# Fused soft-capped attention and maxout layer on one core: row-wise loads of v, a fourth U buffer, the weight product earlier, and the last sums of exp on VectorE

## The chip, the core and the metric

The kernel runs on one core of a Trainium2 chip. The time of a run is the device time of that core, in microseconds (us). A run more than 1.5% above the fastest of the same kernel counts as slow and is left out of ratios. Small differences are read from ratios of many runs; profiles, of which there is one for each kernel, show where time goes. TensorE multiplies matrices, ScalarE does tanh and exp, VectorE and GpSimd add, copy, convert and scale, and SP issues DMAs. The span is the time from the first to the last instruction of a profile, and the granted clock is the share of TensorE's full clock that the profile records.

## The reference, cut to what matters

```python
# q, k, v: (8 batches, 12 heads, 448 tokens, 64), float32
scores = 30 * tanh((q @ k.T) / 8 / 30)
attn = exp(scores) / sum(exp(scores))      # max subtraction cancels; |scores| <= 30
x = (attn @ v)                             # heads side by side: (3584, 768)
out = maximum(x @ w1, x @ w2) @ w_out      # d_ff = 1024, out (3584, 768)
```

The kernel uses max(h1, h2) = h2 + relu(h1 - h2). With wd = w1 - w2 and M = w2 @ w_out, out = x @ M + relu(x @ wd) @ w_out. It computes wd and M itself, in its first third.

## The kernel before

Two heads are one pair (48 pairs), two pairs are one **quad** (24, the loop's `t`), three pairs are one group, for which q, k and v are loaded together. A batch needs three quads. While quad `t` is in its attention part, TensorE also works off **fillers**: single matmuls of the second stage, taken from a queue with `F(n)`. A batch of 132 or 160 such matmuls (`moe(b)`) enters the queue when the rows of that batch are normalized. Line numbers in profiles are those of the kernel that ran; after the change most are 5 higher (`L396` becomes `L401`).

```python
def F(n):                        # let up to n fillers out
    while n > 0 and fill_q: ...  # an empty queue loses the quota

def pv(t, ab):                   # attn @ v of one pair, and the sums of exp
    ...
    if ab:
        ss = pv_psum.tile([P, 512], f32, name="ss")
        for m in range(2):
            nc.tensor.matmul(ss[64 * m : 64 * m + 64, :S], ones2, expo[t, 2][:, m, :],
                             start=True, stop=False)                       # L340
        nj = NJ if t < NS else 1
        for j in range(nj):
            for m in range(4):   # 12 matmuls before quad NS; 4 on VectorE's sums (esum) from NS on
                x = e_of(t, m // 2, j)[:, m % 2, :] if t < NS else esum[t][:, m, :]
                nc.tensor.matmul(ss[32 * m : 32 * m + 32, :S], ones, x,
                                 start=False, stop=(j == nj - 1))          # L347
    ...
    if ab == 0:
        U[t] = upool.tile([P, 2, S], f32, name="u", bufs=3)
    nc.vector.tensor_copy(U[t][:, ab, :], ps[:, :S])                       # L351

def normalize(t, ab, eng=nc.gpsimd):     # xT = U * 1/sum, on GpSimd       # L383
    ...

for t in range(NQ):
    i = 2 * t
    weights(i)                           # M: turn_w2 and premultiply enter the queue, from MS on
    if t % 3 == 2 and t > 2:
        fill_q.append(moe(t // 3 - 1))   # its first matmuls, L396, read xT of quads up to t - 3
    scores(t + 1, 0); ex(t, 3)
    F(2); add(t, 0, 1); F(2)             # add: sums of exp on VectorE
    ...
    F(5 + more8 if more else 0)
    if t > 4: spread(t - 2)              # 1/sum back from memory (rec_b), on the SP queue
    extra(i)                             # loads (SP), casts (GpSimd), DMA transposes (SP) of later groups
    F(6 if more else 3)
    scores(t + 1, 1); ex(t + 1, 0)
    pv(t, 0)
    F(8 + more8); F(3 if more else 0)
    if MS < i <= MS + KC: subtract(i - MS - 1)    # wd
    if t > 4: normalize(t - 2, 0); normalize(t - 2, 1)
    ...
```

A denominator goes a long way: sums on TensorE, copy (VectorE), DMA, reciprocal (VectorE), DMA to memory (`rec_d`), DMA back to all rows (`rec_b`), multiplication on GpSimd (`xT`). All these DMAs are issued by SP, in order, among the loads of q, k, v and the transposes. A batch has six chunks `c`, one for each pair; its first matmuls read chunks 0 to 3, so only four of them can run if the last quad of the batch isn't normalized.

## Time and profile before

| | before |
|---|---|
| median of the runs at hand before the prediction | 376.99 us (376.53 to 381.85, 3 runs) |
| profiled run | 380.94 us, span 379.2 us, granted clock 0.98 |
| TensorE / ScalarE / VectorE / GpSimd busy | 92% / 74% / 53% / 40% |
| ScalarE waits for scores (tanh, L296) | 31.1 us |
| attention part ends (last exp) | about 319 us; then TensorE alone |

A quad needs 11.8 us of ScalarE. What exceeds this in a quad is a wait somewhere. I therefore time quads: from the first matmul of the first `pv` of one quad to that of the next.

Three waits of the kernel before (the view of waits: engine, line, what it waited for; us in total, times, longest):

```profile
POOL kqf L178 <- DMA qr<-in_q_dram: 9.4, 9, 2.2
...
PE s L295 <- DMA qkT<-kqf: 2.3, 2, 1.9
PE mm L396 <- POOL xT L383: 1.3, 1, 1.3
```

GpSimd's cast of q (`kqf`) waits 9.4 us in all for its loads and never over 2.2, TensorE's scores wait twice for a DMA transpose (`qkT`), and the first matmuls of a batch wait once for the normalized rows (`xT`).

### The profile page before, as it was taken

To read this page: it belongs to the slowest core of one execution; us is meant where nothing else is said; L and a number is where in the kernel's file an instruction comes from. 1 tells how busy PE (TensorE), PEld (TensorE's weight loads), DVE (VectorE), ACT (ScalarE), POOL (GpSimd) and SP (SyncE) were. 2 spreads that over 40 slices of the span, in tenths; PEclk is the share of its full clock that TensorE was granted. 3 is DMA by queue.
4 is the path that set the end of the run, shared out by engine and by line. 5 is a ranking of instruction groups with operands and counts; after the bars stand their busy time and mean duration, and the time that the engine had idled before them with its cause. 6 is when DMAs were issued, how large, how long until landed. Compare 5 with 4: busy or idle time off the path is not lost.

```text
span 379.2 us, 6549 instructions
## 1 busy us (share of the span) xinstructions
PE 349.0 (92%) x2492; PEld 168.2 (44%) x2492; DVE 200.6 (53%) x348; ACT 281.8 (74%) x265; POOL 150.1 (40%) x188
## 2 busy tenths in 40 slices
PE   3677986898999999999999999999989999999996
PEld 2223443443444444444444454434434444555563
DVE  4223473567665676455745654557448556633421
ACT  4999986697999989998898899889958897000000
POOL 3734135637554445444562456243644302420000
PEclk9997898999999999999999999999989999999999
DMA  7999999996788987999698959896988132422022
GB/s 251 263 209 220 274 284 223 227 193 139 215 212 221 213 232 203 223 234 255 177 213 208 251 163 250 232 242 165 216 217 213 51 91 105 122 80 95 2 83 84
DMA packets 104464, 71.56 MB, mean 189 GB/s; under 512 B 58224, under 2 KB 99440, under 8 KB 104432
## 3 DMA queue, kind: packets, MB, share of 16 engines
q1 hardware_dynamic: 102480, 67.99, 71.1%
q0 software_dynamic: 1952, 3.15, 4.5%
q8 instruction: 19, 0.31, 0.4%
q14 instruction: 13, 0.11, 0.1%
HBM read 53.48 MB, written 11.18 MB: 171 GB/s over the span
## 4 chain that ended last, share of the span: by engine, by line
PE 65%; DMA 19%; DVE 5%; SPq 4%; ACT 3%; issue 2%; POOL 1%; POOLq 0%; DVEq 0%; ACTq 0%
PE mm L396 17%; PE mm L411 16%; PE mm L408 12%; PE pv L334 6%; DMA qkT<-kqf 6%; PE s L295 6%; DMA qr<-in_q_dram 6%; DMA vr<-in_v_dram 4%; DMA rec_b<-rec_d 3%; PE pv L348 3%; PE ss L347 2%; PE s L290 1%; DVE u L351 1%; ACT expo L303 1%; ACT tanh L296 1%
## 5 line engine op out<-in xcount | busy, mean ns | idle before, releaser
L296 ACT ACTIVATE tanh<-s 128x896 bf16<-128x896 f32 x144 | 124.3, 915 | 32.5 <-PE s L295 31.1
L303 ACT ACTIVATE expo<-tanh 128x1792 bf16<-128x1792 bf16 (+1 forms) x96 | 144.9, 1510 | 0.1
L383 POOL TENSOR_TENSOR xT<-u,rec_b 128x448 bf16<-128x448 f32 x48 | 58.4, 1238 | 101.1 <-DMA rec_b<-rec_d 81.2
L411 PE MATMUL mm<-wo_sb,gT 128*128 128x384 bf16 x448 | 86.8, 330 | 0.0
L396 PE MATMUL mm<-xT,wd_sb 128*128 128x448 bf16 x384 | 79.1, 354 | 2.7 <-POOL xT L383 1.3
L351 DVE COPY u<-pv 128x448 f32<-128x448 f32 x48 | 29.9, 624 | 91.0 <-PE pv L348 78.3
L408 PE MATMUL mm<-wm_sb,xT 128*128 128x384 bf16 x336 | 66.6, 326 | 0.2 <-DVE gT L400 0.2
L411 PEld LDWEIGHTS <-gT 128*128 128x128 bf16 x448 | 43.6, 99 | 31.1 <-issue 3.6
L415 DVE COPY osb<-mm 128x384 f32<-128x384 f32 x56 | 31.1, 555 | 46.3 <-PE mm L411 46.0
L396 PEld LDWEIGHTS <-wd_sb 128*128 128x128 bf16 x384 | 37.2, 98 | 38.4 <-issue 5.9
L295 PE MATMUL s<-qkT 64*128 64x448 bf16 x288 | 43.2, 371 | 11.1 <-ACT tanh L298 3.4
L400 DVE TENSOR_SCALAR gT<-mm 128x448 bf16<-128x448 f32 x64 | 39.1, 616 | 16.8 <-PE mm L396 16.6
L408 PEld LDWEIGHTS <-xT 128*128 128x128 bf16 x336 | 32.5, 98 | 23.3 <-issue 1.9
L334 PE MATMUL pv<-expo,vp 128*64 128x448 bf16 x288 | 37.5, 370 | 0.0
L158 POOL CAST vp<-vr 128x1152 bf16<-128x1152 f32 x15 | 18.0, 1201 | 46.8 <-DMA vr<-in_v_dram 43.5
L321 DVE TENSOR_TENSOR esum<-esum,expo 128x896 bf16<-128x896 bf16 x38 | 29.9, 787 | 1.5
L319 DVE TENSOR_TENSOR esum<-expo 128x896 bf16<-128x896 bf16 x38 | 26.6, 699 | 0.0
L295 PEld LDWEIGHTS <-qkT 64*128 64x128 bf16 x288 | 9.4, 95 | 36.8 <-issue 28.7
L298 ACT ACTIVATE tanh<-s 128x896 bf16<-128x896 f32 x24 | 22.0, 917 | 4.4 <-PE s L290 3.9
L334 PEld LDWEIGHTS <-vp 128*64 128x64 bf16 x288 | 12.4, 110 | 21.3 <-issue 15.2
L232 PE MATMUL mm<-wo_sb,w2T 128*128 128x384 bf16 x96 | 19.1, 334 | 1.4 <-DVE qkT L264 1.4
L178 POOL CAST kqf<-qr 128x1152 bf16<-128x1152 f32 x12 | 14.5, 1207 | 9.6 <-DMA qr<-in_q_dram 9.4
(56 smaller groups left out, 227.7 us busy)
## 6 DMA issues: line engine op xcount, KB each, us to landing
rec_b<-rec_d SPq DMA_DIRECT2D x48, 224.0 KB
kr<-in_k_dram SPq DMA_DIRECT2D x12, 576.0 KB
qr<-in_q_dram SPq DMA_DIRECT2D x12, 576.0 KB
vr<-in_v_dram SPq DMA_DIRECT2D x12, 576.0 KB
out_dram<-osb SPq DMA_DIRECT2D x17, 384.0 KB
out_dram<-osb SPq DMA_DIRECT2D x22, 192.0 KB
osb<-in_moe_w_dram SPq DMA_DIRECT2D x6, 512.0 KB
vr<-in_v_dram SPq DMA_DIRECT2D x8, 288.0 KB
```

Source lines behind the costliest of these rows:

```text
L295: nc.tensor.matmul(s[:, h, :S], k0[r, j * P : (j + 1) * P], qTn[r, :])
L296: nc.scalar.activation(tanh[t, p][:, 2 * m : 2 * m + 2, :], s[:, :, :S], AF.Tanh, scale=scale / cap)
L303: nc.scalar.activation(expo[t, p], tanh[t, p][:, 0:n, :], AF.Exp, scale=float(cap))
L321: nc.vector.tensor_add(d, d, e_of(t, ab, 0 if ab else 2))
L334: nc.tensor.matmul(ps[r, :S], vp[g % 2][:, 2 * n + h, j, :], e_of(t, ab, j)[:, h, :], start=(j == 0), stop=False)
L351: nc.vector.tensor_copy(U[t][:, ab, :], ps[:, :S])
L383: eng.tensor_mul(xT[b // 2][:, hp, cs], U[t][:, ab, :], rec[t][:, ab, :])
L396: nc.tensor.matmul(ps[:, :S], wd_sb[:, c, f * P : (f + 1) * P], x[:, c, cs], start=(c == 0), stop=(c == KC - 1))
L400: nc.vector.tensor_relu(g[:, f, cs], ps[:, :S])
L408: nc.tensor.matmul(ps[:, : DM // 2], x[:, c, ts], wm_sb[:, c, hs], start=(c == 0), stop=False)
L411: nc.tensor.matmul(ps[:, : DM // 2], g[:, f, ts], wo_sb[:, f, hs], start=False, stop=(f == FC - 1))
L415: nc.vector.tensor_copy(osb[:, hs], ps[:, : DM // 2])
```

## The change

Its intent: take matmuls from TensorE (the sums of the tokens left over, 64 of 448, of both pairs), take away the stall of VectorE at the third U tile, finish M and the first batch sooner, have the transposes of even groups half a quad earlier, and load v of the first groups in longer rows. The diff, cut to its core:

```diff
-        if g < NT and what == "v":          # 4 DMAs per group: gone; the cast sorts the rows
[...]
-        if step == 0:
+        if step == 2:                        # left tokens of a pair: 64 partitions
+            r = slice(64 * ab, 64 * ab + 64)
+            d = esum[t][r, ab::2, :]
+            nc.vector.tensor_add(d, d, expo[t, 2][r, :, :])
+        elif step == 0:
[...]
-            for m in range(2):
+            for m in range(2 if t < NS else 0):
[...]
-            U[t] = upool.tile([P, 2, S], f32, name="u", bufs=3)
+            U[t] = upool.tile([P, 2, S], f32, name="u", bufs=4)
[...]
-    NS = 5
+    NS = 2
[...]
-            at(e - 4, cross, g)              # DMA transpose of group g
+            at(e - 4 if g % 2 or first else e - 5, cross, g)
[...]
-    MS = 3
+    MS = 2                                   # and the loads of w1, w2 sooner
[...]
-        if t % 3 == 2 and t > 2:
+        if t % 3 == 2 and t > 5:
             fill_q.append(moe(t // 3 - 1))
[...]
-        if t > 4:
+        if t > 3:
             spread(t - 2)                    # likewise normalize, half a quad sooner for quad 2
[...]
+        if t == 4:                           # in the middle of quad 4
+            fill_q.append(moe(0))
[...]
+        add(t, 0, 2)
         F(2 + more8 if more else 0)
-        add(t, 1, 0)
+        add(t, 1, 2)
```

## The prediction

> **What bounds the kernel now.** I read the page first, then the chain of waits, then the idle times of ScalarE and VectorE in order of time, then the PE timeline of the end.
>
> The page and the groups of instructions:
>
> ```profile
> PE 349.0 (92%) x2492; PEld 168.2 (44%) x2492; DVE 200.6 (53%) x348; ACT 281.8 (74%) x265; POOL 150.1 (40%) x188
> PE   3677986898999999999999999999989999999996
> ACT  4999986697999989998898899889958897000000
> L296 ACT ACTIVATE tanh<-s 128x896 bf16<-128x896 f32 x144 | 124.3, 915 | 32.5 <-PE s L295 31.1
> L321 DVE TENSOR_TENSOR esum<-esum,expo 128x896 bf16<-128x896 bf16 x38 | 29.9, 787 | 1.5
> L340 PE MATMUL ss<-expo,ones 128*64 128x448 bf16 x48 | 8.8, 362 | 0.0
> ```
>
> There are two stages. Until the last exp (319 us) ScalarE is almost full; then TensorE alone works off what is left of the second product (319 to 376 us). ScalarE's own pace in a stretch without gaps (148.63 to 160.42 us in the timeline) is 11.8 us for a quad (two head pairs). From the first pv matmul of quad 5 (90.30 us) to that of quad 22 (309.32 us) a quad takes 219.0/17 = 12.9 us, so about 1.05 us per quad, 18 us in all, is ScalarE waiting for scores because TensorE has not come to them. Before that the largest gaps are in quads 3 to 5. ScalarE's timeline, and VectorE's and TensorE's at the same places (the bracket is the idle time before and what ended it):
>
> ```profile
> 63.33 0.62 DVE L351 COPY u<-pv 128x448 f32<-128x448 f32 x1 [5.60 <-POOL xT L383]
> 67.98 1.73 ACT L296 ACTIVATE tanh<-s 128x896 bf16<-128x896 f32 x2 [4.26 <-PE s L295]
> ...
> 76.11 1.73 ACT L296 ACTIVATE tanh<-s 128x896 bf16<-128x896 f32 x2 [1.45 <-PE s L295]
> ...
> 90.28 1.73 ACT L296 ACTIVATE tanh<-s 128x896 bf16<-128x896 f32 x2 [2.14 <-PE s L295]
> ```
>
> ```profile
> 277.61 0.55 PE L295 MATMUL s<-qkT 64*128 64x448 bf16 x4 [1.85 <-DMA qkT<-kqf]
> 278.08 1.73 ACT L296 ACTIVATE tanh<-s 128x896 bf16<-128x896 f32 x2 [2.33 <-PE s L295]
> ...
> 283.00 1.73 ACT L296 ACTIVATE tanh<-s 128x896 bf16<-128x896 f32 x2 [1.62 <-PE s L295]
> ```
>
> The first says: the copy of quad 3's product into its U tile stood 5.6 us until GpSimd had normalized quad 0, because there are three U tiles; VectorE is in order, so TensorE's evacuations stood behind it, then the scores, then ScalarE. The second: the DMA transpose of an even group came late, TensorE stood 1.85 us, and ScalarE lost 2.33 and then 1.62 us. Smaller gaps behind transposes of even groups are 0.62 us (161.04) and 0.93 us (237.98).
>
> **What the Trainium skill says.** "VectorE: DVE Perf Modes", The perf-mode tier table: a two-input bf16 op in SBUF runs at two elements per cycle, and the page measured some 150 cycles fixed cost; for 896 elements (150 + 448)/0.96 GHz = 0.62 us, an estimate. The trace agrees: undisturbed adds take 0.61 to 0.62 us; the means of 699 and 787 ns hold adds of up to 1.55 us, in stretches where GpSimd was at work. It also says that lanes run in parallel along the free dimension, so an add on 64 partitions should cost the same as one on 128; no view of this kernel has one. "TensorEngine Tiling (Array Packing)", Key Properties: changing the tiling mode drains TensorE. The trace agrees in this: a pair of 64-column sum matmuls ought to stream 448 columns at 2.4 GHz, 0.19 us, but takes 0.29 us from start to start of the next group. "TensorE: Matmul & The Clock Gate", Part 1: an idle TensorE falls to half clock. After the 1.85 us stall, 8 matmuls of L411 take 2.56 us in the chain, against 1.30 us elsewhere; this is why one late transpose cost ScalarE twice. "DMA: Bandwidth & Descriptors", Specifications: under 512 bytes a transfer is below line rate. The page shows 58224 of 104464 packets under 512 bytes, with the DMA share at 0.94 to 1.14 in the first 60 us; the trace doesn't show how much of that the size of the packets costs.
>
> **The change part by part.** The end of the attention stage:
>
> ```profile
> 315.23 0.76 PE L334 MATMUL pv<-expo,vp 128*64 128x448 bf16 x6
> 315.82 0.36 PE L340 MATMUL ss<-expo,ones 128*64 128x448 bf16 x2
> 316.11 0.37 PE L347 MATMUL ss<-esum,ones 128*32 128x448 bf16 x4
> 316.42 0.36 PE L348 MATMUL pv<-expo,vl 128*128 128x448 bf16 x1
> ```
>
> *Sums on VectorE.* L340 is gone for quads 2 to 23: 316.11 - 315.82 = 0.29 us of TensorE each. In quads 2, 3, 4 the twelve L347 matmuls (82.25 to 82.94 us, 0.69 us) become four (0.31 us), 0.38 us more each. Together 22 x 0.29 + 3 x 0.38 = 7.5 us of TensorE. VectorE gets 2 adds of 0.62 to 0.79 us in 22 quads, and 4 more in quads 2 to 4: 56 adds, 35 to 44 us; it goes from 201 to about 240 us, 65% of the span. Where does this lie? In quads 5 to 22 TensorE is the later one, by about 0.4 us in a quad of L408 and L411 matmuls (12.2 us against 11.8) and 1.3 to 1.8 us in one of L396 (13.2 to 13.6 us; each of the 48 fillers takes 0.189 instead of 0.163 us). So 0.29 us per quad counts in full in some 14 quads (those from 8 on): 4 us. VectorE has the room: in the densest stretch (168 to 171 us, an L396 quad) one extra add falls between the evacuations and the sum matmul; the last add ended at 170.12 us and would end about 170.8 us, the sum matmul stands at 171.25 us. If GpSimd stretches adds to 1.1 us, half a microsecond is lost; I take off 1 us over all these quads. In quads 2 and 3 it is tighter: per quad 2 subtractions (2.5 us), 2 w2T and 4 wm copies (3.6), 2 qkT copies (1.3), U, sums and reciprocal (2.3) make 9.7 us, and six adds of 0.75 us make 14.2 us against 11.8 us of ScalarE. I expect 1 to 2 us lost in each.
>
> *Four U tiles.* Takes away the 5.6 us stall of VectorE, so ScalarE's 4.26 us and the cold clock's 0.81 us behind it. With a fourth tile the copy of quad 4 (at 77.29 us) meets a normalization finished at 63.3 us: hidden.
>
> *M sooner.* I counted fillers from the loop: TensorE's quotas that find an empty queue are 82 before (44 in quad 0, 36 in 1, 2 in 2) and 76 after (44, 18, and 14 in quad 7, where the second batch can't begin before quad 8). So the tail has 295 matmuls in place of 301: 6 x 0.163 = 1.0 us. The first L396 matmul moves from quad 5 to the second half of quad 4, and so does its wait for the normalization of quad 2. Before, this and the last wd_sb, wm_sb waits cost 2.14 us in quad 5 and 1.45 us at 76 us; since the spread of the sums also moves half a quad ahead, I expect about 1.5 us to remain of these 3.6.
>
> *Transposes of even groups half a quad ahead.* Removes 2.33 + 1.62 + 0.62 + 0.93 = 5.5 us at best; the SP queue is in order and stands behind sums and casts, so I count 4.
>
> *v in 1792-byte rows.* For four groups 4 DMAs become 1, and 1152 packets (768 of 768 bytes, 384 of 256) become 384. At the mean 42 ns per packet (71.1% of 16 x 379 us over 102480 packets) the old way is an estimated 3.0 us of all engines per group; the new packets are longer, so perhaps 0.5 us is saved per group. ScalarE waits for no v load from 11 to 54 us, so little reaches the end. The casts get dearer: GpSimd 4 x about 0.66 (from 64x192 in 0.35 us and 64x384 in 0.50 us) + 2 x 0.35 = 3.3 us instead of 1.8, three times, in a stage where it works some 6 of 20 us; on VectorE about 1 us more at 17 us. I count this part as 0, within 0.5 us.
>
> Sum: 5 (U) + 2 (first L396) + 4 (transposes) + 4 - 1 (sums in steady state) + 1 (tail) + about 0.5 (last quad) - 3 (VectorE in quads 2, 3) = 12.5 us. Not all such gaps add up, since removing one lets the next wait come forward; I keep 11: 377 - 11 = 366 us.
>
> **Rivals.** (1) VectorE becomes what TensorE waits for, through the two mm banks and the sum matmul that now waits for six adds. For it: the adds stretched to 1.55 us, and the 14.2 us in quads 2 and 3; against it: 53% busy, and gaps of 0.4 to 1.3 us in each quad of the timeline. It would give back 5 to 8 us: about 372. (2) ScalarE's pace takes it all: whatever TensorE saves is hidden behind tanh and exp. For it: at 100 to 130 us ScalarE has no gap. Against it: 18 us of gaps after quad 5. If only the U stall and the transposes were won: about 368. (3) The SP queue and the DMAs: the earlier transpose blocks the loads and sums behind it, and a stall only moves. For it: SP waits of 31 us for rec_d and 12 us for casts of q, and DMA at 0.8 to 1.0. It would leave about 371. (4) Everything works, and the wait for the first L396 vanishes: about 361.
>
> **Range and chances.** 80%: 360 to 373. The threshold for faster is 377 x 0.98 = 369.4; rivals 1 and 3 land above it, the sum itself well below. Faster 0.72, within 2% 0.25, slower 0.03 (it would need VectorE to lose more than all gaps hold).
>
> **What would show it.** L340 with only 4 matmuls, and sums in quads 2 to 4 shorter; adds on VectorE near 132 with a mean of 0.7 to 0.8 us; no U copy waiting for xT near 63 us; ScalarE's waits for scores down from 31 to 17 to 20 us; the last exp at about 308 instead of 319 us; the tail 1 us shorter; no wait for qkT at quad 20. Wrong, if VectorE's waiting shows as new idle time of TensorE ("DVE esum", "DVE gT") of over 3 us, or if ScalarE's gaps stay near 30 us.

## More of the kernel before

Runs of one kernel differ by a few microseconds: the kernel before took between 375.5 and 384.7 us in all its runs, on several chips.

Since the loop puts scores and fillers of quad t before `pv(t, 0)`, a batch that enters at the top of quad 8 begins in what is timed as quad 7.

## The result, and the profile after

| | before | after |
|---|---|---|
| median | 377.60 us (376.53 to 381.85, 4 runs) | 390.81 us (389.89 to 395.53, 4 runs) |
| ratio of fast runs, 95% interval | | 1.0353 (1.0238 to 1.0469): slower |
| profiled run | 380.94 us, span 379.2 | 389.89 us, span 388.1 |

A ratio is the mean time of one kernel's fast runs over that of the other's of the same rounds, so it is not quite the ratio of the medians that stand beside it.

The page of the kernel after: busy times, TensorE and ScalarE in 40 slices of the span, and the groups that answer to those of before:

```profile
PE 348.1 (90%) x2424; PEld 165.7 (43%) x2424; DVE 249.8 (64%) x407; ACT 281.7 (73%) x265; POOL 162.9 (42%) x197
...
PE   4677877688999499999999999999999999899996
...
ACT  4999985837899859998899899998997897000000
...
L296 ACT ACTIVATE tanh<-s 128x896 bf16<-128x896 f32 x144 | 124.3, 914 | 40.2 <-PE s L295 39.1
...
L326 DVE TENSOR_TENSOR esum<-esum,expo 128x896 bf16<-128x896 bf16 x44 | 37.0, 842 | 2.1
...
L322 DVE TENSOR_TENSOR esum<-esum,expo 64x896 bf16<-64x896 bf16 x44 | 34.9, 793 | 0.9
L324 DVE TENSOR_TENSOR esum<-expo 128x896 bf16<-128x896 bf16 x44 | 33.1, 752 | 0.0
```

TensorE is busy for about as long as before and stands longer. VectorE has 49 us more. ScalarE waits 39.1 us for scores in place of 31.1. The slices, 9.7 us each, show where: a trough in slices 6 to 10 (49 to 97 us), where ScalarE has 8, 5, 8, 3 and 7 tenths and TensorE 7, 7, 6, 8 and 8; a single 4 of TensorE in slice 14 (126 to 136 us) with ScalarE's 5 behind it; then 9s of TensorE almost throughout.

The share of each engine in the chain that ended last, of the kernel before:

```profile
PE 65%; DMA 19%; DVE 5%; SPq 4%; ACT 3%; issue 2%; POOL 1%; POOLq 0%; DVEq 0%; ACTq 0%
```

And of the kernel after:

```profile
PE 69%; DVE 19%; ACT 5%; DMA 3%; issue 2%; POOL 1%; SPq 0%; DVEq 0%; POOLq 0%
```

VectorE, which was 5% of the chain, is 19% of it. DMA, which was 19%, is 3%: the chain runs no longer through loads, but through adds and copies. The quads, in us, from the starts of the pv matmuls:

| quad | 2 | 3 | 4 | 5 | 7 | 13 | 14 | 19 | 20 | last pv at |
|---|---|---|---|---|---|---|---|---|---|---|
| before | 12.87 | 18.53 | 14.17 | 12.59 | 11.98 | 12.36 | 13.65 | 15.85 | 14.11 | 319.0 |
| after | 17.70 | 19.51 | 14.48 | 13.10 | 17.46 | 12.74 | 13.31 | 13.46 | 13.43 | 327.7 |

The spans differ by 388.1 - 379.2 = 8.9 us: +1.5 up to the start of quad 2, +5.8 in quads 2 and 3, +0.6 in quads 4 to 6, +5.5 in quad 7, -4.7 in quads 8 to 22, +0.2 after that. So there are two holes and a gain behind them.

**The first hole, quads 2 and 3.** One stretch of each kernel, two quads long (columns: stretch; length; busy us and number of instructions of TensorE, its weight loads, VectorE, ScalarE, GpSimd; granted clock; DMA share; GB/s). Beside after I set the experiment e3 below, which has the four U tiles but no adds in these quads, since the kernel before has its U stall here. Of after:

```profile
46.19:83.40 37.21, 27.81 (x263) 13.27 (x261) 28.23 (x40) 23.55 (x23) 22.66 (x24) 0.88 0.69 200
```

And of e3:

```profile
44.27:70.89 26.62, 23.81 (x280) 12.05 (x278) 17.25 (x27) 23.67 (x24) 14.33 (x16) 1.00 1.04 276
```

VectorE's 28.2 us are just the 2 x 14.2 us that the prediction had counted. But the two quads took 37.2 us and not 28.2. Compare e2 below, which differs from e3 in the adds alone (VectorE 29.95 us in 36.15 us): of 12.7 us more work on VectorE 9.5 us came through as length, although e3's VectorE had 9.4 us idle. TensorE's timeline of after says why (each line: start, length, engine, line, operation, and in the bracket the idle time before it and what ended it):

```profile
54.38 0.37 PE L352 MATMUL ss<-esum,ones 128*32 128x448 bf16 x2 [1.51 <-DVE esum L326]
...
59.89 0.60 PE L262 MATMUL mm<-ident,kqf 64*64 64x64 bf16 x26 [2.52 <-DVE wm_sb L237]
...
68.97 1.46 PE L232 MATMUL mm<-wo_sb,w2T 128*128 128x384 bf16 x8 [1.48 <-DVE qkT L264]
...
76.99 0.60 PE L262 MATMUL mm<-ident,kqf 64*64 64x64 bf16 x26 [2.62 <-DVE w2T L224]
```

TensorE stands for a sum, and for copies (`wm_sb`, `qkT`, `w2T`) that stand in VectorE's order behind adds and subtractions; then it is VectorE that waits for TensorE's next product (in the same stretch 3.6 us for L232, 3.8 us for pv), and the idle times of the two add up. The granted clock falls too: it is 0.50 from 60.53 to 63.94 us and from 77.60 us to the end of the stretch, 0.88 on average, where e3 has 1.00; in the first of these, 6 matmuls of L232 take 2.08 us in place of 1.14. One add shows how long such a stand can be; VectorE and GpSimd in the timeline, and then ScalarE's gap:

```profile
73.63 2.70 DVE L324 TENSOR_TENSOR esum<-expo 128x896 bf16<-128x896 bf16 x1
73.64 2.21 POOL L388 TENSOR_TENSOR xT<-u,rec_b 128x448 bf16<-128x448 f32 x2
...
83.19 1.73 ACT L296 ACTIVATE tanh<-s 128x896 bf16<-128x896 f32 x2 [6.30 <-PE s L295]
```

The add took 2.70 us where one alone takes 0.61. It began within 0.01 us of GpSimd's two normalizations and ended, at 76.33 us, 0.48 us after the second of them (73.64 + 2.21 = 75.85 us). It is the longest add of the profile; what all such blocking costs was not measured.

**The second hole, quad 7.** SP, GpSimd, TensorE and ScalarE in order of time:

```profile
119.39 4.51 SPq L268 DMA_TRANSPOSE qkT<-kqf  x1
123.96 0.57 SPq L125 DMA_DIRECT2D qr<-in_q_dram  x1
...
129.39 1.15 POOL L178 CAST kqf<-qr 128x1152 bf16<-128x1152 f32 x1 [5.66 <-DMA qr<-in_q_dram]
...
133.04 2.22 POOL L388 TENSOR_TENSOR xT<-u,rec_b 128x448 bf16<-128x448 f32 x2 [1.58 <-DMA rec_b<-rec_d]
...
134.22 0.53 PE L401 MATMUL mm<-xT,wd_sb 128*128 128x448 bf16 x1 [2.26 <-POOL xT L388]
135.31 4.07 PE L401 MATMUL mm<-xT,wd_sb 128*128 128x448 bf16 x11 [0.56 <-POOL xT L388]
...
139.77 1.73 ACT L296 ACTIVATE tanh<-s 128x896 bf16<-128x896 f32 x2 [4.92 <-PE s L295]
```

A transpose holds SP for 4.51 us; the load of q comes behind it, and so do the sums and rec_b; GpSimd stands 5.66 us for q, then for rec_b; and TensorE, which has just begun the second batch, has nothing else to do and stands 2.26 and 0.56 us. Its clock is low as well: the granted clock is 0.50 from 132.21 to 139.04 us, and 11 matmuls take 4.07 us (11 of the 13 in a row take 2.24 us in e18 below). It fell 0.25 us into the first of these waits, after 3.41 us in which TensorE had been busy for 1.83. ScalarE loses 4.92 us. The waits of after, in the same form as those of before:

```profile
POOL kqf L178 <- DMA qr<-in_q_dram: 26.7, 9, 5.7
...
PE mm L401 <- POOL xT L388: 3.7, 4, 2.3
```

No wait for `qkT <- kqf` by DMA is left on TensorE. In its place GpSimd waits 26.7 us for q and TensorE 3.7 us for xT.

### The profile page after: what moved, and what is told of

Same layout as the page of the kernel before. It is cut to its first block, busy times and chain, and to the rows that moved or that the text cites.

```text
span 388.1 us, 6456 instructions
## 1 busy us (share of the span) xinstructions
PE 348.1 (90%) x2424; PEld 165.7 (43%) x2424; DVE 249.8 (64%) x407; ACT 281.7 (73%) x265; POOL 162.9 (42%) x197
## 4 chain that ended last, share of the span: by engine, by line
PE 69%; DVE 19%; ACT 5%; DMA 3%; issue 2%; POOL 1%; SPq 0%; DVEq 0%; POOLq 0%
PE mm L416 17%; PE mm L401 14%; PE mm L413 13%; PE s L295 7%; PE pv L339 7%; PE pv L353 3%; DVE esum L322 3%; DVE esum L324 3%; DVE esum L326 2%; ACT expo L303 2%; PE mm L232 2%; PE ss L352 2%; ACT tanh L296 2%; DVE u L356 2%; DVE gT L405 2%
## 5 line engine op out<-in xcount | busy, mean ns | idle before, releaser
L296 ACT ACTIVATE tanh<-s 128x896 bf16<-128x896 f32 x144 | 124.3, 914 | 40.2 <-PE s L295 39.1
L388 POOL TENSOR_TENSOR xT<-u,rec_b 128x448 bf16<-128x448 f32 x48 | 60.5, 1280 | 91.2 <-DMA rec_b<-rec_d 80.8
L401 PE MATMUL mm<-xT,wd_sb 128*128 128x448 bf16 x384 | 81.8, 359 | 6.5 <-POOL xT L388 3.7
L295 PE MATMUL s<-qkT 64*128 64x448 bf16 x288 | 44.0, 376 | 11.3 <-DVE qkT L264 4.8
L405 DVE TENSOR_SCALAR gT<-mm 128x448 bf16<-128x448 f32 x64 | 39.1, 614 | 16.6 <-PE mm L401 16.2
L326 DVE TENSOR_TENSOR esum<-esum,expo 128x896 bf16<-128x896 bf16 x44 | 37.0, 842 | 2.1
L339 PE MATMUL pv<-expo,vp 128*64 128x448 bf16 x288 | 37.5, 369 | 0.0
L322 DVE TENSOR_TENSOR esum<-esum,expo 64x896 bf16<-64x896 bf16 x44 | 34.9, 793 | 0.9
L324 DVE TENSOR_TENSOR esum<-expo 128x896 bf16<-128x896 bf16 x44 | 33.1, 752 | 0.0
L178 POOL CAST kqf<-qr 128x1152 bf16<-128x1152 f32 x12 | 14.5, 1208 | 27.0 <-DMA qr<-in_q_dram 26.7
L158 POOL CAST vp<-vr 128x1152 bf16<-128x1152 f32 x12 | 14.9, 1246 | 23.9 <-DMA vr<-in_v_dram 20.4
L232 PE MATMUL mm<-wo_sb,w2T 128*128 128x384 bf16 x96 | 21.3, 360 | 2.9 <-DVE qkT L264 2.9
```

The costliest lines, as they stand in the source:

```text
L295: nc.tensor.matmul(s[:, h, :S], k0[r, j * P : (j + 1) * P], qTn[r, :])
L296: nc.scalar.activation(tanh[t, p][:, 2 * m : 2 * m + 2, :], s[:, :, :S], AF.Tanh, scale=scale / cap)
L322: nc.vector.tensor_add(d, d, expo[t, 2][r, :, :])
L324: nc.vector.tensor_add(d, e_of(t, ab, 1 if ab else 0), e_of(t, ab, 2 if ab else 1))
L326: nc.vector.tensor_add(d, d, e_of(t, ab, 0 if ab else 2))
L339: nc.tensor.matmul(ps[r, :S], vp[g % 2][:, 2 * n + h, j, :], e_of(t, ab, j)[:, h, :], start=(j == 0), stop=False)
```

## The experiments

Three first suspicions, lettered in the expectations where letters are used: **A**, the adds from quad 2 on take too much of VectorE while M is prepared; **B**, M and the first batch come before their inputs; **C**, the earlier transposes hold up the SP queue. Two more came up on the way: **E**, the order of SP's issues is what makes xT late; **F**, what decides is how many fillers of the previous batch are left when a batch begins. The median before in each row is over all runs of the kernel before in the same batch of runs on that chip; the ratio uses those of the same rounds. Each edit is given against the kernel named.

| run | median us (range, runs) | before us | ratio (95%) |
|---|---|---|---|
| e1 | 390.32 (387.68 to 393.63, 4) | 379.79 | 1.0219 (1.0141 to 1.0297) |
| e2 | 387.05 (386.72 to 387.56, 4) | 379.79 | 1.0157 (1.0087 to 1.0226) |
| e3 | 378.76 (376.81 to 384.15, 20) | 379.79 | 1.0010 (0.9979 to 1.0040) |
| e4 | 388.96 (387.57 to 395.24, 4) | 379.79 | 1.0194 (1.0122 to 1.0267) |
| e5 | 379.22 (375.43 to 383.29, 20) | 379.29 | 0.9965 (0.9935 to 0.9996) |
| e6 | 381.60 (377.90 to 385.56, 20) | 379.29 | 1.0056 (1.0028 to 1.0084) |
| e7 | 379.49 (376.12 to 383.79, 12) | 379.29 | 1.0010 (0.9971 to 1.0050) |
| e8 | 380.39 (378.09 to 383.95, 20) | 379.29 | 1.0032 (1.0004 to 1.0059) |
| e9 | 396.88 (393.90 to 573.32, 4) | 379.28 | 1.0456 (1.0368 to 1.0545) |
| e10 | 381.64 (379.86 to 387.15, 8) | 379.28 | 1.0072 (1.0030 to 1.0114) |
| e11 | 385.55 (383.93 to 390.14, 4) | 379.28 | 1.0169 (1.0117 to 1.0221) |
| e12 | 386.07 (381.32 to 386.95, 4) | 379.28 | 1.0172 (1.0098 to 1.0245) |
| e13 | 397.33 (396.82 to 403.17, 4) | 378.52 | 1.0513 (1.0449 to 1.0578) |
| e14 | 395.43 (382.85 to 398.72, 4) | 378.52 | none: only one fast run |
| e15 | 388.87 (385.81 to 397.56, 4) | 378.52 | 1.0267 (1.0181 to 1.0353) |
| e16 | 388.15 (381.36 to 397.67, 4) | 378.52 | 1.0136 (1.0038 to 1.0233) |
| e17 | 375.09 (372.38 to 379.00, 9) | 378.92 | 0.9895 (0.9856 to 0.9934) |
| e18 | 379.08 (373.54 to 380.85, 12) | 378.92 | 0.9929 (0.9877 to 0.9980) |

All gave correct results. The profiles of e4, e6, e11, e13, e14 and e16 fell on runs that count as slow; of these places are used, and totals only where it is said. The quads of the profiles that the argument uses:

| quad | 2 | 3 | 4 | 7 | 13 | 14 | last pv at |
|---|---|---|---|---|---|---|---|
| e1 | 13.94 | 14.25 | 21.30 | 16.18 | 13.53 | 13.30 | 325.9 |
| e2 | 15.65 | 20.50 | 14.11 | 12.89 | 16.76 | 15.35 | 324.3 |
| e3 | 12.87 | 13.75 | 16.35 | 12.46 | 16.91 | 15.35 | 316.4 |
| e5 | 12.86 | 14.80 | 16.11 | 11.98 | 12.84 | 13.66 | 315.1 |
| e10 | 15.78 | 14.22 | 14.46 | 16.78 | 13.40 | 13.58 | 319.5 |
| e12 | 15.58 | 14.23 | 21.33 | 15.77 | 13.64 | 13.47 | 324.0 |
| e17 | 12.87 | 13.76 | 15.78 | 12.41 | 12.01 | 13.04 | 312.9 |
| e18 | 14.27 | 14.22 | 13.41 | 12.40 | 12.42 | 13.33 | 311.5 |

### Undoing parts: e1 to e4

**e1, the adds only from quad 5 on.** Against after:

```diff
-    NS = 2
+    NS = 5
```

> The changed kernel, but the sums of exp go to VectorE from quad 5 on, as before, not from quad 2 (18 adds fewer, in the stage in which M is prepared). Theory A (VectorE is full in quads 2 and 3: the new adds stand in front of the evacuations there): quad 2 falls from 17.7 to about 13.5 us, quad 3 from 19.5 to about 14.5 us, and the time falls by 7 to 9 us, to 382 to 384 us; the loss in quad 7 (17.5 us against 12.0 before) stays. Theory B (the hole in the queue of fillers and the late xT in quad 7 are the whole loss): unchanged within 1.5 us, 389 to 392. Theory C (the order of the SP queue, with the transposes of even groups ahead, makes the loads late): unchanged too.

The first hole is gone, 14.25 + 13.94 = 28.2 us in place of 37.2, but little of the time comes back (1.0219 in place of 1.0353, in other rounds): quad 4 takes 21.3 us. TensorE and ScalarE in the timeline of e1:

```profile
82.20 0.41 PE L401 MATMUL mm<-xT,wd_sb 128*128 128x448 bf16 x1 [4.85 <-POOL xT L388]
...
84.78 1.73 ACT L296 ACTIVATE tanh<-s 128x896 bf16<-128x896 f32 x2 [6.23 <-PE s L295]
```

The first batch, which now enters in the middle of quad 4, reaches its matmuls long before quad 2 is normalized. In after, VectorE's slowness had hidden this: there no matmul waits for xT in quad 4. The time that was expected back was missed: undoing one cause of a hole uncovered the other.

**e2, M as before.** Against after: every hunk for M taken back (`MS = 3`, the loads of w1 and w2, `moe(0)` at the top of quad 5, spread and normalize).

```diff
-    MS = 2
+    MS = 3
[...]
-        if t == 4:
-            fill_q.append(moe(0))
```

> The changed kernel, but M is prepared when it was before, and the first batch of the second product begins in quad 5 as before (MS 3, loads of w1 and w2, subtractions, spread and normalization of the first quads as before). Theory B: the 5.5 us in quad 7 go away, and the time falls to about 385 us. Theory A: VectorE stays overfull, since sums from quad 2 on still fall into the preparation of M; quads 2 to 4 together stay near the 51.7 us of after (45.6 before), so no more than 5 us are won there. If both hold: 381 to 386 us. Theory C: unchanged, 389 to 392.

Quad 7 is down to 12.89 us; quads 2 and 3 stay at 36.2 us, in a fast run. The time, 387.05 us, lies just above the 381 to 386 that were expected. So the second hole belongs to M and the first to the adds.

**e3, both.** Against e2: `NS = 5`. What is left of the change is four U tiles, the rows of v, the earlier transposes and the left sums on VectorE from quad 5 on.

```diff
-    NS = 2
+    NS = 5
```

> Both taken back: M as before and sums of all tokens on VectorE from quad 5 on; what stays of the change is v in 1792-byte rows, four U tiles, the left tokens' sums on VectorE from quad 5 on, and the transposes of even groups ahead. Theories A and B together: no loss is left, and the gains of the prediction remain (U stall about 4 to 5 us, left tokens and transposes 4 to 6 us): 367 to 372 us, faster than the kernel before. Theory C: still slower than before, above 380 us.

Both holes are gone (26.6 us in quads 2 and 3, 12.46 in quad 7), and yet the ratio is 1.001. The remaining parts, for which I had expected some 10 us, brought nothing that the end shows. In this profile TensorE waits 2.94 us for xT at 201.92 us, at the start of batch 3, and quads 13 and 14 take 32.3 us in place of 26.0 before.

From e3 the costs of the two other parts can be worked out: the adds from quad 2 on cost 1.0157 / 1.001, 1.5%, without M sooner, and 1.0353 / 1.0219, 1.3%, with it; M sooner costs 1.0219 / 1.001, 2.1%, or 1.0353 / 1.0157, 1.9%. They look additive, but each ratio of 4 runs is uncertain by about 0.8% on either side, and that of after is from other rounds than the rest.

**e4, transposes as before.** Against after: the whole hunk with `first` taken back (transposes of even groups, and the first shifted loads and casts).

```diff
-            at(e - 4 if g % 2 or first else e - 5, cross, g)
+            at(e - 4, cross, g)
```

> The changed kernel, but loads, casts and transposes of the groups from the fifth on at the places of before. Theory C: the loss goes, below 380 us. Theories A and B: the time stays or rises by up to 4 us, to 390 to 395 us, because the late transpose in quad 19 comes back.

The ratio, 1.0194, is below both that after got (1.0353, and 1.0456 in e9), but those are from other rounds, and the first interval overlaps. A gain of 1 to 2% from taking the transposes back is therefore neither shown nor excluded here. What is excluded is that they are the whole loss: the time stays far above 380 us. In the profile no wait for xT is left on TensorE, and there are four waits for transposes, 8.7 us in all, one of them 2.60 us in quad 7. Without M and the early adds, e7 and e8 below show no gain from taking them back beyond 0.3%. The earlier transposes exchange one wait for another.

### Parts alone: e5 to e8

**e5, four U tiles alone.** Against before:

```diff
-            U[t] = upool.tile([P, 2, S], f32, name="u", bufs=3)
+            U[t] = upool.tile([P, 2, S], f32, name="u", bufs=4)
```

> The kernel before with four U tiles and nothing else. The U stall at quad 3 is its own cause: quad 3 falls from 18.5 to 13 to 14.5 us, the time by 3 to 5 us (ratio about 0.989). Rival: the stall only moves to the first L396 matmuls in quads 4 and 5, as in the run before this call, where quad 4 took 16.4 us: then 0 to 2 us (ratio 0.995 to 1.0).

The stall is gone: quad 3 falls from 18.53 to 14.80 us. Of these 3.7 us quad 4 takes 1.9 back (14.17 to 16.11), because TensorE now comes to the first batch before quad 2 is normalized: it waits for xT 2.5 us in all in place of 1.3. Over 20 runs 0.35% is left, 1.3 us.

**e6, left sums on VectorE from quad 5 on, alone.** Against before: the hunks of `add`, `pv` and the order of adds, with `NS = 5` kept.

```diff
+        if step == 2:
+            ...
-            for m in range(2):
+            for m in range(2 if t < NS else 0):
```

> The kernel before with the left tokens' sums on VectorE, but from quad 5 on, and nothing else. If TensorE's 0.29 us per quad count: quads 9, 10, 12, 15, 16, 18 at 12.0 us instead of 12.2 to 12.7, quads of L396 not longer: 3 to 5 us less (ratio about 0.99). If VectorE is what TensorE waits for in the steady state: same or up to 3 us more.

It is slower, by 0.56%, where 3 to 5 us less had been hoped for. Undisturbed quads do get shorter (9 and 15: 12.01 in place of 12.20 us), but by 0.19 and not 0.29 us; and in the profile, of a slow run, the DMA transposes come late more often, 5.2 us in three waits in place of 2.3 in two.

**e7, no M, no transposes.** Four U tiles, rows of v, left sums from quad 5: e3 without the earlier transposes.

```diff
-            at(e - 4 if g % 2 or first else e - 5, cross, g)
+            at(e - 4, cross, g)
```

> The kernel with M and the first sums as before (378.8 us, quads 13 and 14 at 32.3 us in sum), and now the transposes of even groups as before too; left of the change: v rows, four U tiles, left tokens' sums from quad 5 on. Theory D (a transpose issued half a quad sooner holds the SP queue for 4.7 us in front of a load of q; the cast of q then holds GpSimd in front of a normalization, and the next batch's first matmuls wait for xT): quads 13 and 14 fall to 25 to 27 us and the time to 371 to 375 us, unless the late transpose of quad 19 comes back, 374 to 377 us. Rival (quads 13 and 14 were chance, or come from the sums): 377 to 380 us.

The same 1.001 as e3, where 371 to 377 us had been expected; the time goes into other waits: 5.5 us for transposes (four), 1.2 us for xT, and quads 13 and 14 at 28.1 us.

**e8, earlier transposes alone.** Against before, the whole hunk that e4 takes back.

```diff
-            at(e - 4, cross, g)
+            at(e - 4 if g % 2 or first else e - 5, cross, g)
```

> The kernel before with the transposes of even groups half a quad ahead and nothing else. The prediction's step (the late transposes of quads 10, 16 and 19 go away): 3 to 5 us less. Theory D: the loss moves to a load of q and a normalization, quad 13 or 14 gets 3 to 6 us longer: 0 to 3 us more than before.

The waits of e8, to be set beside those of before:

```profile
POOL kqf L178 <- DMA qr<-in_q_dram: 26.0, 10, 5.3
...
PE mm L396 <- POOL xT L383: 5.9, 6, 1.8
```

The 2.3 us of waits for transposes are gone, and 4.6 us more of waits for xT have come. GpSimd stands 26.0 us for q in place of 9.4, and the normalizations, which follow in GpSimd's order, are late with it: the chain that quad 7 of after shows, with the transpose ahead of the load of q on SP. The time is 0.3% longer, and the part for which the prediction had counted 4 us gives nothing.

### Why M and the adds cost: e9 to e12

**e9, the changed kernel once more**, on another chip, unedited.

> The changed kernel unaltered, to have it in the same rounds as the runs beside it and a second trace of it. Ratio to before 1.028 to 1.036; quads 2, 3 and 7 again the long ones (17 to 20, 17 to 20, 15 to 18 us), the other places shifted by chance.

Three fast runs took 393.90, 394.24 and 399.51 us, so the ratio is above the first one. The fourth took 573.32 us at a mean granted clock of 0.575, and the profile fell on it: it says nothing of the rest.

**e10, first batch at the top of quad 5.** Against e1; M stays sooner.

```diff
-        if t % 3 == 2 and t > 5:
+        if t % 3 == 2 and t > 2:
[...]
-        if t == 4:
-            fill_q.append(moe(0))
```

> The run with sums from quad 5 on (390.3 us, quad 4 21.3 us, quad 7 16.2 us), with one thing more taken back: the first batch of the second product enters the queue at the start of quad 5, not in the middle of quad 4; M is still prepared early. The 14 quotas without work then fall into quad 4, not 7. Theory M1 (what the early M costs is that L396 matmuls are reached before their xT is there, and TensorE is in order): quad 4 falls to 14 to 16.5 us, quad 7 to 12 to 13.5 us, the time to 379 to 383 us, ratio 1.000 to 1.008. Rival (the early loads of w1 and w2 delay the other loads, and that is the cost): ratio stays at 1.017 or more.

Quad 4 falls from 21.30 to 14.46 us and the ratio from 1.0219 to 1.0072. So 1.5 of M's 2.1% are the half quad by which the first batch came too soon. Quad 7 stays at 16.78 us, which I had not expected: TensorE waits for xT there, 1.74 and 1.12 us, as in after.

**e11, adds that nobody reads.** Against e3: the six adds of quads 2 to 4 run, into their own tile, but the sums are still taken by twelve matmuls.

```diff
-        if t < NS or t >= NQ:
+        if t < 2 or t >= NQ:
             return
```

> The kernel with M and the first sums as before (378.8 us, ratio 1.001), but VectorE also makes the six adds in quads 2, 3 and 4, into a tile that TensorE does not read; the sums there stay with TensorE's matmuls, so the result is right. Theory A1 (VectorE's time is what is short in quads 2 and 3: evacuations stand behind the adds): quads 2 and 3 grow from 26.6 to 34 us or more, the ratio to 1.014 or more, like the run with only M taken back (1.0157). Theory A2 (the sum matmuls wait for the last add, and TensorE is in order): quads 2 and 3 stay below 29 us, ratio below 1.006.

Quads 2 and 3 take 81.38 - 44.79 = 36.6 us in place of 26.6 (a slow run; e2, in a fast one, has 36.2), and the ratio of fast runs goes from 1.001 to 1.0169, some 6 us. No matmul waits for the sums of these adds, so it is VectorE's time and order that cost. The largest wait of TensorE in e11 is again for a copy:

```profile
PE mm L262 <- DVE wm_sb L237: 5.6, 1, 5.6
```

**e12, twenty unread matmuls in the hole.** Against e1: a filler that only keeps TensorE busy, queued behind batch 0, where the queue runs empty in quad 7.

```diff
+    def idle_mm(n):
+        ps = mm_psum.tile([P, 512], f32, name="mm")
+        for _ in range(n):
+            nc.tensor.matmul(ps[:, :S], wd_sb[:, 0, :P], xT[0][:, 0, :S], start=True, stop=True)
+            yield
[...]
             fill_q.append(moe(0))
+            fill_q.append(idle_mm(20))
```

> The run with sums from quad 5 on, with 20 matmuls behind the first batch whose result nobody reads (14 fill the hole in quad 7, 6 stand before the second batch in quad 8, as the rest of the first batch did before). Theory M2 (the hole leaves TensorE cold and lets the second batch reach its xT too soon): quad 7 falls from 16.2 to 12 to 13.5 us, the time by 2 to 4 us against that run (ratio about 1.012); quad 4 stays at 20 to 22 us. Rival (xT is late by more than the six matmuls cover): quads 7 and 8 together stay at 29 us or more, ratio unchanged.

Quad 7 hardly changes, 15.77 in place of 16.18 us: TensorE is no longer idle before the batch, but it still waits 2.40 and 0.74 us for xT inside it. 14 of the 20 went out in the quotas that the empty queue had lost, and only 6 were left to cover a delay of some 3 us. An idle TensorE just ahead of the batch is not the cause; the late xT is. Nor is the half clock: in e12 the granted clock is 1.00 throughout quad 7.

### The order on SP: e13 to e16

If xT is late because loads and rec_b stand in one queue, changing their order should help.

**e13, loads before rec_b.** Against e3:

```diff
+        extra(i)
         if t > 4:
             spread(t - 2)
-        extra(i)
```

> The kernel with M and the first sums as before (378.8 us), but in the first half of a quad the loads are issued before the two rec_b DMAs, so SP does not hold loads back while it waits for rec_d (31 to 37 us of waiting in all). Theory E (SP's order paces the steady state): GpSimd's waits for loads of q (5 to 7 us each) shrink, and the time falls by 2 to 6 us, ratio 0.985 to 0.995. Rival (the DMA engines' load, not the order of issue, makes them late): same within 0.4 per cent; rec_b then only comes later, xT too, and it could be 1 to 3 us slower.

It is much worse, 1.0513. TensorE waits for xT eight times, 17.8 us in all, for instance in batch 3:

```profile
213.11 0.53 PE L401 MATMUL mm<-xT,wd_sb 128*128 128x448 bf16 x1 [4.38 <-POOL xT L388]
```

So rec_b must not stand behind loads; the order that the kernel has is the better one.

**e14, e15 and e16, rec_b issued by GpSimd.** The same order, and rec_b on GpSimd's own queue; against e3, e10, and (with four U tiles) e6.

```diff
-            nc.sync.dma_start(
+            nc.gpsimd.dma_start(
                 out=rec[t][64 * h : 64 * h + 64, :, :], in_=lines[h : h + 1, :, :].to_broadcast([64, 2, S])
```

> As the run before, but the rec_b DMAs are issued by GpSimd's queue, after the casts: SP loses 24 x 1.25 us of issue and its waits for rec_d, GpSimd pays for the descriptors (0.5 to 0.8 us each in the trace for w2 and wo, so 24 to 38 us over the span, of 150 busy). Theory E: 3 to 7 us faster than with SP, ratio 0.98 to 0.993. Rival: GpSimd's casts and normalizations come later by its waiting for rec_d, ratio 1.0 to 1.02.

> The run with M early and the first batch in quad 5 (ratio 1.0072, quad 7 16.8 us), with rec_b from GpSimd's queue after the loads. In that run SP issued rec_b of quad 5 4.5 us into quad 7, against 1.6 us where M is late and quad 7 takes 12.5 us. Theory E: rec_b of quad 5 is issued sooner, quad 7 falls to 12 to 13.5 us, ratio 0.985 to 0.997. Rival (the wait for rec_d itself is the length of the chain, whoever issues): quad 7 stays above 15 us.

> The kernel before with four U tiles and left sums from quad 5 on, v, M and transposes as before, and rec_b from GpSimd's queue after the loads. Theory E: the late transposes (DMA qkT waits of 1 to 3 us in quads 13, 16 and 19) go, ratio 0.98 to 0.992. Rival: they stay, ratio 0.995 to 1.01.

In all three the loads also come ahead of rec_b in the loop, as in e13, so two things differ from what they came from. All are worse than that, as far as they can be compared: e14 has one fast run, 382.85 us, e15 1.0267 against 1.0072, e16 1.0136. TensorE waits for xT 17.3, 12.9 and 12.1 us. Moving rec_b off SP doesn't help. That GpSimd's own order, with its casts that wait for q, is what holds rec_b there, is likely but no run isolates it; rec_b ahead of the casts was not tried. These four runs failed as remedies.

### How much is left when a batch begins: e17 and e18

For every kernel the loops tell how many fillers of the previous batch are left when a batch enters:

| batch | 0 | 1 | 2 | 3 | 4 | 5 | 6 | matmuls after the last quad |
|---|---|---|---|---|---|---|---|---|
| before | 6 | 6 | 22 | 10 | 26 | 14 | 30 | 301 |
| after | 4 | 0 | 16 | 4 | 20 | 8 | 24 | 295 |
| e17 | 6 | 21 | 37 | 25 | 41 | 29 | 45 | 316 |
| e18 | 0 | 21 | 37 | 25 | 41 | 29 | 45 | 316 |

In the profiles of before, after and the first sixteen experiments TensorE's waits for xT stand at the starts of batches 0, 1, 3 and 5, with 0 to 14 left. Where 16 or more are left there is none, except two in e14 and e16, where rec_b itself was delayed. Few left doesn't always mean a wait (e4 has none), but every wait met few left. A filler takes 0.163 to 0.189 us, so 21 of them cover 3.4 to 4.0 us, about the lateness of xT. The next two runs hold back 15 (e17) and 21 (e18) fillers in quads 5 to 7, so that later batches begin with more, at the price of as many in the tail.

**e17.** Against e3:

```diff
-        F(6 if more else 3)
+        F(1 if 5 <= t <= 7 else 6 if more else 3)
```

> The kernel with M and the first sums as before (ratio 1.001; its trace waits 2.9 us for xT at batch 3, and quads 13 and 14 take 32.3 us), with 5 fillers fewer in each of quads 5, 6, 7, so that 21, 25 and 29 matmuls in place of 6, 10 and 14 are left when batches 1, 3 and 5 begin; 15 matmuls (15 x 0.163 = 2.4 us) move to the tail. Theory F (a batch's first matmuls come before the last normalization they need, because too little of the batch before is left): no wait for xT at batches 1, 3, 5; quads 13 and 14 take 25 to 27 us; ratio 0.986 to 0.995. Rival (xT is late because the stage is paced by the DMAs, and the wait comes whenever): waits for xT or qkT of 2 us or more stay after quad 6, ratio 1.003 to 1.010.

The ratio goes from 1.001 to 0.9895. TensorE no longer waits for xT or a transpose at all, and quads 13 and 14 take 25.1 us in place of 32.3. Quads 5 to 7, from which the fillers were taken, are no shorter (37.6 us, 37.5 in e3), so the gain is not there. ScalarE's waits for scores in e17:

```profile
ACT tanh L296 <- PE s L295: 26.1, 35, 4.9
```

Of the 31.1 us of before 26.1 are left, as predicted for the change in kind but not in size. The kernel with four parts of the change and this one line is 1.05% faster than the kernel before (0.66 to 1.44%), with an interval that lies below 1, and so ahead of both kernels. Its 15 fillers more in the tail are an estimated 15 x 0.163 = 2.4 us, which this gain has already paid.

**e18.** Against e10, which has M sooner:

```diff
-        F(6 if more else 3)
+        F(0 if 5 <= t <= 7 else 6 if more else 3)
[...]
-        F(5)
+        F(4 if 5 <= t <= 7 else 5)
```

> The run with M early and the first batch in quad 5 (ratio 1.0072, quad 7 16.8 us, no matmul left at batch 1), with 7 fillers fewer in each of quads 5, 6, 7: 21, 25 and 29 are left at batches 1, 3, 5, and the tail has 21 matmuls (3.4 us) more. Theory F: quad 7 falls to 11.5 to 13 us, ratio 0.993 to 1.001. Rival: quad 7 stays at 15 us or more, ratio 1.010 or more.

Quad 7 falls from 16.78 to 12.40 us and the ratio from 1.0072 to 0.9929 (of 12 runs six count as slow and are not in it; the means of all runs would give 0.998, so this gain hangs on the cut, while that of e17 does not: 0.991). TensorE in quad 7, and the next gap of ScalarE:

```profile
126.80 2.62 PE L401 MATMUL mm<-xT,wd_sb 128*128 128x448 bf16 x13
...
132.91 1.73 ACT L296 ACTIVATE tanh<-s 128x896 bf16<-128x896 f32 x2 [0.53 <-PE s L295]
```

The matmuls of the second batch now run at full clock, and no wait stands before them. That answers what e10 and e12 had left open: the second hole is the empty backlog at batch 1, which leaves a late xT uncovered.

## Why the prediction was wrong

It said 366 us, 360 to 373; the kernel took 390.81. One of its own signs of being wrong came true: ScalarE's waits for scores did not fall to 17 to 20 us but rose to 39.1. Its own terms, set against the two profiles by stage:

| stage | predicted, us | measured, us |
|---|---|---|
| up to quad 2 | 0 | +1.5 |
| quads 2 and 3 | -5 (U) + 3 (VectorE) = -2 | +5.8 |
| quads 4 to 7 | -2 (first batch) | +6.1 |
| quads 8 to 22 | -4 + 1 (sums), -4 (transposes) = -7 | -4.7 |
| quad 23 and the tail | -1.5 | +0.2 |
| sum | -12.5 | +8.9 |

**Mis-sized: "- 3 (VectorE in quads 2, 3)".** The mechanism was named, with its 14.2 us per quad, and the trace has 28.2 us for both quads, exactly that. The step that failed is from busy time to duration: "1 to 2 us lost in each" took the quad to last about as long as its fullest engine works. It lasted 18.6 us on average. VectorE and TensorE take turns through two PSUM banks (the two `mm` buffers for TensorE's products), each in its own order, so an add in front of a copy makes TensorE stand, and afterwards VectorE stands for TensorE. e2 and e11 measure the term, 9.5 and 10.0 us more for two quads (some 6 us at the end) where 3 were put down, and e11 shows that of the two ways that rival 1 named, the mm banks and the sum matmul that waits for six adds, the first is enough: in e11 no matmul waits for the sums of these adds. Rival 1 also had the size, 5 to 8 us, nearer. A second thing was missing. The Trainium skill, "SBUF — State Buffer", Who interferes with whom, says that a VectorE instruction with two SBUF inputs contends with a GpSimd instruction that reads SBUF, and that the one that comes second fully blocks. The trace agrees that one blocks the other: the add of 2.70 us is one of 0.61 us that stood beside two normalizations of together 2.21 us. On the order it doesn't agree as it reads, since the add is recorded 0.01 us ahead of the first of them; such a difference may be within the error of the records. The prediction had put the longest at 1.55 us and worked with a mean of 0.75 us.

**Failed: "2 (first L396)" and "1 (tail)".** The prediction gave the earlier batch only its benefit. It saw that the wait for the first product would come in quad 4, and expected "about 1.5 us to remain". In after that is what remained (1.39 us for `wm_sb` at 90.53 us, none for xT), but only because VectorE was late itself; without that, e1 has 4.85 us for xT there, and e1 to e10 puts the step at 1.5% of the time. It also counted "14 in quad 7" among the lost quotas and used them only for the length of the tail. These 14 meant that batch 1 would begin with no filler left, so that a late xT stops TensorE (2.26 and 0.56 us in after, in a quad 5.5 us longer). e18, which keeps M sooner and 21 fillers, shows this: quad 7 falls by 4.4 us against e10. Work was shifted to the front, where its inputs were not there yet. Nor did the six matmuls fewer in the tail show: from the first pv of quad 23 to the end it takes 60.4 us in place of 60.2.

**Failed: "5 (U)" and "4 (transposes)" as gains of the end.** Each stall went, as predicted: no copy of U waits for xT any more, no transpose is waited for at quad 20. But e5 gains 0.35% and e8 loses 0.3%. The prediction subtracted gaps of ScalarE one by one and then took off 1.5 us for "the next wait"; in fact the next wait stood directly behind: e5 gave back half of it at batch 0, and e8 exchanged waits for transposes for waits for xT. Rival 3 had the mechanism ("a stall only moves") and the queue, SP; it let such waits eat 5 us of the gain, and in e3 and e7 all of it is gone.

**About right: the steady state, "4 - 1" and the transposes.** From quad 8 on after gains 4.7 us of the 7. An undisturbed quad gains 0.19 us from the left sums in e6, not 0.29: the prediction took the 0.29 us between the starts of L340 and L347 as what L340 costs, but from the last `pv` matmuls to L352 there are then 0.10 us more (0.69 us from L339 to L352, 0.59 from L334 to L340), so that much, which the prediction itself had put down to the change of tiling, stays. An add on 64 partitions takes as long as one on 128 (median 0.62 us for both), as expected. The mean of the adds, 105.0 us / 132 = 0.795 us, lies at the upper end of what was predicted. Alone, though, the left sums make the kernel 0.56% slower (e6); that an earlier TensorE without backlog then meets its inputs too soon is likely, but not shown for e6.

**v in rows: "0, within 0.5 us"** was not tested alone. e7 is e5 and e6 together with these rows: 1.0010 against 0.9965 x 1.0056 = 1.0021 leaves -0.1% for the rows, an estimate that is uncertain by 0.4% and more; the packets under 512 bytes fell from 58224 to 56496.

**What stays open.** The +1.5 us up to quad 2 is in after, but not in e1 (quad 2 starts at 44.54 us) nor in e2 (44.26, before 44.73), so neither M nor the adds bring it alone; e4, which has both, begins quad 2 at 47.57 us, in a slow run. Why after was 1.0353 on one chip and 1.0456 on another isn't known. And the loss in quads 2 and 3 was not split into what VectorE's order costs and what the blocking by GpSimd costs: taking GpSimd's work out of these quads wasn't tried.

## What to carry to other kernels

When two engines feed each other through a few buffers in order, more work on one of them can lengthen the stage even where it looks idle (here 9.5 us for 12.7 us of work, with 9.4 us idle before); measure such a stage with dummy work before moving more onto it. Before starting a batch of work sooner, ask whether its last input is there and how much other work is left to cover it if it is late: here one line that held back 15 matmuls turned a change of no effect (1.001) into a gain of 1% (0.9895). A removed stall counts only down to the next wait behind it, so find that wait first, and don't add up the gaps.

## What the Trainium skill lacked or had wrong

- "SBUF — State Buffer": it says that the loser of the shared ports waits for the whole instruction. It doesn't say that the loser can stay blocked over two GpSimd instructions in a row: the add at 73.63 us took 2.70 us beside two of together 2.21 us, and by the records it had begun first.
- "TensorE: Matmul & The Clock Gate", Part 1: its table ties the fall to half clock to at least one idle window of about 3.4 us. Here TensorE need not be idle that long: in after the granted clock fell at 132.21 us, and TensorE had been busy for 1.83 of the 3.41 us before; in the kernel before it fell at 279.04 us, after 3.41 us with 1.56 busy and a single wait of 1.85 us (8 matmuls in 2.56 us against 1.30).
- "DMA: Bandwidth & Descriptors": apart from cycle counts for earlier chip generations in a comparison with trn3, no section gives the time for which a DMA transpose holds the queue that issues it. On SP it was 4.3 to 6.1 us in the kernel before, median 4.56, while the part of a q load behind one took 0.57 us there (at 123.96 us of after); this is what made the load of q behind it late.
- No page gives a way to size the mutual waiting of two engines: two quads with 28.2 us of VectorE work took 37.2 us.
